# Other tiles for the first block of x and for the feature DFT weights, and the order of the loads with them

## The chip, the cores and the metric

The kernel runs on one NeuronCore of a Trainium2 chip. What counts is the device time of one execution in microseconds (us). Before the change the median of three runs is 1732.21 us (1732.16 to 1733.36).

The engines are TensorE (PE in the profile; PEld is its weight load), VectorE (DVE), ScalarE (ACT) and GpSimd (POOL). SP (SyncE) computes nothing here: it is the one queue from which every DMA of this kernel is issued, in order, and an instruction that waits there holds back all behind it.

## The reference

The input x has 2048 tokens and 640 features. With g = sigmoid(x . gate_w), one number for each token, the result is g * A(x) + (1 - g) * B(x):

```python
# A: real part of a DFT over the features, then over the tokens
a = einsum("bsd,ed->bse", x, dft_hid_re)
b = einsum("bsd,ed->bse", x, dft_hid_im)
y = einsum("ts,bse->bte", dft_seq_re, a) - einsum("ts,bse->bte", dft_seq_im, b)

# B: attention with 32 query heads of 20, one key and one value head
q = (x @ wq).reshape(B, S, 32, 20).transpose(0, 2, 1, 3)
k, v = x @ wk, x @ wv
p = softmax(einsum("bhqd,bkd->bhqk", q, k) * 20 ** -0.5)
o = einsum("bhqk,bkd->bhqd", p, v).transpose(0, 2, 1, 3).reshape(B, S, 640) @ wo
```

All of it is float32.

## The kernel before

**Splits.** A float32 matrix is used as two parts, a high part that TensorE takes fast and the rest. So each loaded tile is *split*: one instruction copies the high part and one subtracts it. In the stage of this change, x and `wq` are split on ScalarE (the copy) and VectorE (the subtraction, `xl` in line 375 and `wql` in line 118); the feature DFT weights `wrT` and `wiT` are split on GpSimd, two instructions for each of two parts (lines 211 and 212). A product is three matmuls (lines 122 to 124).

**The first stage.** It takes the first 100 us or so. The tokens are cut into four blocks of 512 (n = 0 to 3), and the 640 features into five chunks (c) of 128. For each block the stage makes keys, values and the gate's input (`kv`, line 396), then the queries of five groups of heads (`q`, m = 0 to 4). `kv_out` (lines 398 to 412) adds up `kvT`, splits the keys and has them written into `ks` by six small DMAs. `q_out` (lines 382 to 389) splits a bank of queries into `qh` and `ql` and has both stored to DRAM, 256 KB each. There are three buffers of `qh` and three of `ql`, so the fourth `q_out` of a block waits for stores of the first to land. After each `q_out` the split of a chunk of the block after next follows (line 479), and in places some score tiles (`a`, line 251) whose maximum VectorE takes (`mx`, line 258).

In block 0, loads, splits and matmuls go chunk by chunk. Then x of block 1 is loaded and split, `kv_out` and the five `q_out` of block 0 follow, and the loop over blocks 1 to 3 begins. In it, `kv_out` of a block stands on ScalarE and VectorE behind the five `q_out` of the block before, and TensorE needs the bank that it frees for the third group of queries.

**Tiles of x.** `load_x1` takes a tile for a whole block from a pool with two buffers (`xr`): blocks 0 and 2 in one, 1 and 3 in the other. So x of block 2 waits until the last chunk of block 0 is split, and block 3 until the last of block 1.

**Tiles of the DFT weights.** `load_w(i, e)` loads half e of `wrT` (i = 0) or `wiT` (i = 1) in two parts of 480 and 320 KB into two staging tiles that `raw_tile` deals out in turn (`raw0`, `raw1`); chunks 2 and 3 of `wq` used them before, and `xraw`, the x of the second stage (320 KB a tile), uses them after. In the first stage the calls for e = 0 stand at the end of blocks 1 and 2.

**What sets the order.** The instructions of TensorE, ScalarE, VectorE and GpSimd run in the order in which they are written. SP's do not: a scheduler places the DMAs by its own estimate of when tiles come free, and gives a tile whichever buffer of its pool is free first by that estimate. So a load written late can stand early on SP, and hold back what is written before it. `DMAHW0` to `DMAHW7` are eight semaphores that the DMAs take in turn, so that a DMA also waits for the one eight places ahead of it to land.

After the first stage come the products with the feature DFT weights beside score tiles, then the long loop of attention and token DFT, and the output product.

Of the kernel before, what the change touches and what calls it, by code (L numbers as in the profile page):

```python
# [8 lines left out]
F32 = mybir.dt.float32  # L9
F32R = mybir.dt.float32r  # L10
AF = mybir.ActivationFunctionType
ALU = mybir.AluOpType
# [5 lines left out]
P = 128  # L18
# [4 lines left out]
KC = D // P  # L23
# [3 lines left out]
HALF = D // 2  # L27
SJ = NT // 2
SCALE = float(DH) ** -0.5
ROW = 512  # L30
# [3 lines left out]
def kernel(  # L34
# [13 lines left out]
    nc = tc.nc  # L48
# [61 lines left out]
    def words(ap):  # L110
        return ap.bitcast(F32) if ap.dtype == F32R else ap

    def move(dst, src):
        nc.sync.dma_start(words(dst), words(src))  # L114
# [22 lines left out]
    xT_v = xT.rearrange("(c p) t -> p c t", p=P)  # L137
# [18 lines left out]
    def load_qs0(n):  # L156
        if n == 0:
            qs[0] = qbuf[0]
        ts = slice(n * ROW, (n + 1) * ROW)
        for hh in range(2):  # L160
            r = slice(hh * DH, (hh + 1) * DH)
            for k, src in enumerate((qh_d, qh_d, ql_d)):
                b = 64 * hh + 20 * k
                move(qs[0][b : b + 20, ts], src[r, ts])
# [9 lines left out]
    def c_slot(n, shape, dt, name):  # L174
        return cpool.tile(shape, dt, tag=f"c{n}", name=name)
# [6 lines left out]
    def raw_tile(shape, name):  # L182
        nraw["n"] += 1
        k = nraw["n"] % (5 if yp else 2)
        if k >= 2:
            return yp[0].tile(shape, F32, tag=f"raw{k}", name=name, bufs=1)
        return cpool.tile(shape, F32, tag=f"raw{k}", name=name)
# [2 lines left out]
    w_now = {}  # L190
    w_raw = {}

    def load_w(i, e):
        v = (wrT, wiT)[i].rearrange("(c p) n -> p c n", p=P)
        es = slice(e * HALF, (e + 1) * HALF)
        parts = []
        for k, cs in enumerate(CPART):
            shape = [P, cs.stop - cs.start, HALF]
            if k == 0:
                h, l = [c_slot(2 * i + z, shape, F32R, f"w{i}{'hl'[z]}") for z in range(2)]  # L200
            elif i == 1:
                h, l = [c_slot(4 + z, shape, F32R, f"wb{'hl'[z]}") for z in range(2)]
            else:
                h, l = [xp.tile(shape, F32R, name=f"wb{'hl'[z]}0") for z in range(2)]
            raw = raw_tile(shape, "wraw")
            move(raw, v[:, cs, es])
            parts.append((h, l, raw))
        w_raw[i] = parts
# [138 lines left out]
    with ExitStack() as c1:  # L347
        w1 = c1.enter_context(tc.tile_pool(name="w1", bufs=1, side="right"))
        x1 = c1.enter_context(tc.tile_pool(name="x1", bufs=2, side="right"))
# [9 lines left out]
        xs, xsp = {}, {}  # L359

        def load_x1(n, c):
            if n < 4:
                if c == 0:
                    xs[n] = x1.tile([P, KC, ROW], F32, name="xr")
                move(xs[n][:, c], xT_v[:, c, n * ROW : (n + 1) * ROW])

        def split_x1(n, c):
            if n < 4:
                if c == 0:
                    xh = x1.tile([P, KC, ROW], F32R, name="xh")  # L370
                    xl = x1.tile([P, KC, ROW], F32R, name="xl")
                    xsp[n] = (xh, xl)
                xh, xl = xsp[n]
                nc.scalar.activation(xh[:, c], xs[n][:, c], AF.Copy)
                nc.vector.tensor_tensor(xl[:, c], xs[n][:, c], xh[:, c].bitcast(F32), op=ALU.subtract)

        def q_mm(ps, n, m, c):
            ms = slice(m * P, (m + 1) * P)
            xh, xl = xsp[n]
            mm3(ps, wqh[:, c, ms], wql[:, c, ms], xh[:, c], xl[:, c], KC, c)  # L380

        def q_out(ps, n, m):
            ms, ts = slice(m * P, (m + 1) * P), slice(n * ROW, (n + 1) * ROW)
            qh = x1.tile([P, ROW], F32R, name="qh", bufs=3)
            ql = x1.tile([P, ROW], F32R, name="ql", bufs=3)
            nc.scalar.activation(qh, ps, AF.Copy)
            nc.vector.tensor_tensor(ql, ps, qh.bitcast(F32), op=ALU.subtract)
            move(qh_d[ms, ts], qh)
            move(ql_d[ms, ts], ql)

        def kv_mm(ps, n, c):
            xh, xl = xsp[n]
            end = c == KC - 1
            for high in (not end, end):
                m, x = (105, xh) if high else (41, xl)
                nc.tensor.matmul(ps[:m], kvgs[:, c, :m], x[:, c], start=(c == 0 and high), stop=(end and high))
# [17 lines left out]
        def kv_turn(kvT, n, rot):  # L414
            ps = rot(f"kvt_{n}")
            for j in range(4):
                nc.tensor.transpose(
                    ps[:, 64 * j : 64 * j + 41], kvT[:, j * P : (j + 1) * P], ident[:41, :41]
                )
            pv = ps.rearrange("p (j c) -> p j c", c=64)[:, :4]  # L420
            ns = slice(4 * n, 4 * n + 4)
            nc.scalar.activation(vsb[:, ns, :DH], pv[:, :, DH : 2 * DH], AF.Copy)
            nc.vector.tensor_copy(
                gz[:, ns].rearrange("p (j o) -> p j o", o=1), pv[:, :, 2 * DH : 2 * DH + 1]
            )
# [13 lines left out]
        for c in range(KC):  # L439
            if c:  # L440
                load_x1(0, c)
            raw = raw_tile([P, D], "wraw") if c in (2, 3) else w1.tile([P, D], F32, name="wraw", bufs=2)
# [15 lines left out]
        kvT = kv_out(pkv, 0)  # L458
        for m in range(KC):
            q_out(pq[m], 0, m)  # L460
        load_qs0(0)
        rot = Rot(["F1", "V", "S0", "F0"])
        slots = {1: (2, 3), 2: range(KC), 3: range(KC)}
        for n in range(1, 4):
            for c in range(KC):
                load_x1(n + 1, c)
            pkv = rot(f"kv_{n}")
            for c in range(KC):
                kv_mm(pkv, n, c)
            kv_turn(kvT, n - 1, rot)  # L470
            kvT = kv_out(pkv, n)
            if n == 3:
                for k in range(2):
                    load_x(k)
            for m in range(KC):
                ps = rot(f"q_{n}_{m}")
                for c in range(KC):
                    q_mm(ps, n, m, c)
                split_x1(n + 1, m)
                q_out(ps, n, m)  # L480
                if (n, m) == (1, 0):
                    load_qs0(1)
                if m in slots[n]:
                    for z in range(4):
                        a_half(z % 2, f"S{1 + z}")
                if (n, m) == (3, 1):
                    kv_turn(kvT, 3, rot)
                    gate_out()
                if n == 3 and m in (2, 3):
                    split_x(m - 2)  # L490
                if (n, m) == (3, 3):
                    load_x(2)
            if n < 3:
                load_w(n - 1, 0)
                split_w(n - 1)


# [100 lines left out]
    op = ctx.enter_context(tc.tile_pool(name="op", bufs=2))  # L598
# [514 lines left out]
    for plan in plans():  # L1113
        n = sum(w[0] == "b" for w in plan) // 4
# [5 lines left out]
        for what in plan:  # L1120
# [15 lines left out]
            elif what[0] == "b":  # L1136
                p, qh, kc = new[nb[g] // 2]
# [66 lines left out]
```

## Time and profile before

| | before |
|---|---|
| median of 3 runs | 1732.21 us |
| the profiled execution, its own time | 1732.34 us |
| its span, first to last instruction | 1730.6 us |
| TensorE busy | 1710.9 us, 99% |
| VectorE busy | 1381.5 us, 80% |
| ScalarE busy | 1251.2 us, 72% |
| GpSimd busy | 1104.3 us, 64% |
| moved by DMA | 261.47 MB |

The rows of the profile read so. A row of a timeline has start and duration in us, the engine, the line, the operation, the tile it writes and the one it reads, shapes, and in brackets the idle time before it and what ended that. Rows of SP are the issues of DMAs, not the transfers. A row of stretches has the stretch, its length, the busy time of PE, PEld, DVE, ACT and POOL with counts, the granted clock of TensorE (1.00 is full), the DMA share and GB/s. A row of waits has who waited, for what, the sum in us, the number of waits and the longest. The chain of waits follows the work that ended last back from the end; its rows are start, duration and what. A PE row's duration overlaps the next one's: the pace is the distance of the starts.

### The profile page before, as it was taken

How to read it: one execution, taken by the hardware profiler on the slowest of the kernel's cores; microseconds unless marked ns; L12 is line 12 of the kernel's file. 1: busy time of each engine (PE TensorE's matmuls, PEld its weight loads, DVE VectorE, ACT ScalarE, POOL GpSimd, SP SyncE). 2: the span in 40 equal slices, each digit the busy share in tenths (PEclk: the TensorE clock that was granted, in tenths of full speed). 3: DMA queues.
4: the chain of work that ended last, by engine and by line, in shares of the span. 5: the costliest groups of instructions: out<-in, count | busy, mean ns of one | idle time of the engine just before them, and what ended most of it. 6: DMA issues, size and time to landing. Idle time of an engine off the chain costs nothing.

```text
span 1730.6 us, 43337 instructions
## 1 busy us (share of the span) xinstructions
PE 1710.9 (99%) x16752; PEld 1239.4 (72%) x16752; DVE 1381.5 (80%) x2290; ACT 1251.2 (72%) x2543; POOL 1104.3 (64%) x921
## 2 busy tenths in 40 slices
PE   8999999999999999999999999999999999999997
PEld 6686777777677777777777777777777777777664
DVE  5787888888888888888888888888888888888813
ACT  4237888888777677777777777777777767678895
POOL 3045556333356658758777887888877764557785
PEclk9999999999999999999999999999999999999999
DMA  8551223222175556545666776655555533143332
GB/s 270 155 168 56 71 79 105 82 73 72 61 227 168 174 169 196 170 156 200 223 215 211 231 236 217 205 187 185 177 173 170 155 112 111 57 127 117 100 100 85
DMA packets 181499, 261.47 MB, mean 151 GB/s; under 512 B 35696, under 2 KB 136304, under 8 KB 181292
## 3 DMA queue, kind: packets, MB, share of 16 engines
q1 hardware_dynamic: 181292, 258.70, 47.2%
q8 instruction: 132, 2.16, 0.5%
q14 instruction: 75, 0.61, 0.1%
HBM read 184.42 MB, written 76.99 MB: 151 GB/s over the span
## 4 chain that ended last, share of the span: by engine, by line
PE 93%; DMA 2%; DVE 2%; issue 1%; ACT 1%; SPq 1%; POOL 0%; POOLq 0%; DVEq 0%; ACTq 0%
PE av L974 27%; PE y_p L782 21%; PE b L962 18%; PE a L251 15%; PE ab L782 7%; PE oo L782 3%; DVE mx L258 1%; PE q L122 1%; PE q L123 1%; SPq L114 1%; PE q L124 1%; ACT pt L970 1%; DMA wraw<-in_wiT_dram 0%; DMA ql_d<-ql 0%; DMA wraw<-in_wq_dram 0%
## 5 line engine op out<-in xcount | busy, mean ns | idle before, releaser
L258 DVE TENSOR_REDUCE mx<-a 128x1 f32<-128x512 f32 x2048 | 1303.2, 686 | 246.6 <-PE a L251 197.4
L970 ACT ACTIVATE pt<-b 128x512 f32<-128x512 f32 x2048 | 1058.2, 623 | 342.8 <-PE a L251 262.3
L962 PE MATMUL b<-qs,ks 62*128 62x512 f32 x2048 | 755.4, 408 | 3.1 <-ACT pt L970 2.1
L251 PE MATMUL a<-ks,qs 60*128 60x512 f32 x2048 | 707.7, 408 | 2.2 <-DVE mx L258 2.2
L782 PE MATMUL y_p<-tb,ch 64*128 64x320 f32 x3584 | 618.6, 307 | 0.0
L782 PEld LDWEIGHTS y_p<-tb,ch 64*128 64x128 f32 x3584 | 504.3, 186 | 2.9
L974 PE MATMUL av<-pt,vsb 128*32 128x512 f32 x4096 | 485.8, 598 | 0.0
L962 PEld LDWEIGHTS b<-qs,ks 62*128 62x128 f32 x2048 | 345.5, 185 | 187.7 <-DVE mx L258 125.1
L782 PE MATMUL y_p<-tb,cl 64*128 64x320 f32 x1792 | 454.8, 306 | 0.0
L251 PEld LDWEIGHTS a<-ks,qs 60*128 60x128 f32 x2048 | 345.6, 185 | 16.0 <-issue 4.0
L782 PEld LDWEIGHTS y_p<-tb,cl 64*128 64x128 f32 x1792 | 297.2, 186 | 2.7
L974 PEld LDWEIGHTS av<-pt,vsb 128*32 128x32 f32 x4096 | 111.5, 109 | 239.6 <-issue 229.9
L543 POOL TENSOR_TENSOR cl<-craw,ch 128x1024 fp32r<-128x1024 f32 x112 | 268.5, 2397 | 9.0
L824 POOL TENSOR_TENSOR yt<-yt,yu 128x320 f32<-128x320 f32 x86 | 75.0, 872 | 285.3 <-ACT yu L819 232.2
L824 POOL TENSOR_TENSOR abt<-abt,abu 128x320 f32<-128x320 f32 x64 | 55.8, 872 | 198.0 <-ACT abu L819 183.9
L537 POOL TENSOR_TENSOR craw<-craw 128x1024 f32<-128x1024 f32 x64 | 153.4, 2397 | 0.0
L542 POOL CAST ch<-craw 128x1024 fp32r<-128x1024 f32 x112 | 116.6, 1041 | 13.5 <-DMA craw<-in_cre_dram 6.9
L782 PE MATMUL oo<-wo,osp 64*128 64x320 f32 x816 | 91.5, 307 | 0.0
L782 PEld LDWEIGHTS oo<-wo,osp 64*128 64x128 f32 x816 | 86.6, 185 | 1.5
L569 POOL TENSOR_TENSOR tb<-braw,tb 128x320 fp32r<-128x320 f32 x80 | 69.9, 880 | 0.0
L782 PE MATMUL ab<-wbh,xh 64*128 64x320 f32 x256 | 60.1, 306 | 0.0
L782 PE MATMUL ab<-wbh,xl 64*128 64x320 f32 x256 | 59.9, 306 | 0.0
(138 smaller groups left out, 1622.8 us busy)
## 6 DMA issues: line engine op xcount, KB each, us to landing
craw<-in_cre_dram SPq DMA_DIRECT2D x80, 512.0 KB
craw<-in_cim_dram SPq DMA_DIRECT2D x64, 512.0 KB
s_d<-craw SPq DMA_DIRECT2D x32, 512.0 KB
craw<-s_d SPq DMA_DIRECT2D x32, 512.0 KB
braw<-b_d SPq DMA_DIRECT2D x80, 160.0 KB
xraw<-in_xT_dram SPq DMA_DIRECT2D x32, 320.0 KB
b_d<-abt SPq DMA_DIRECT2D x64, 160.0 KB
t_d<-braw SPq DMA_DIRECT2D x64, 160.0 KB
```

Source lines behind the costliest of these rows:

```text
L114: nc.sync.dma_start(words(dst), words(src))
L251: nc.tensor.matmul(ps, qs[v][b : b + 60, qb * P : (qb + 1) * P], ks[b : b + 60, c * ROW : (c + 1) * ROW], start=True, stop=True,)
L258: nc.vector.tensor_reduce(mx[v][:, hh, qb, c : c + 1], ps, axis=AX.X, op=ALU.max)
L537: nc.gpsimd.tensor_tensor(x, raw[0], x, op=how)
L542: nc.gpsimd.tensor_copy(h, x)
L543: nc.gpsimd.tensor_tensor(l, x, h.bitcast(F32), op=ALU.subtract)
L569: nc.gpsimd.tensor_tensor(t[:, 1], raw, t[:, 0].bitcast(F32), op=ALU.subtract)
L782: nc.tensor.matmul(ps, w, x, start=start, stop=stop)
L824: nc.gpsimd.tensor_tensor(t0, t0, t1, op=ALU.add)
L962: nc.tensor.matmul(ps, ks[b : b + 62, kc * P : (kc + 1) * P], qs[NPAIR * (qc // 2) + p][b : b + 62, (qc % 2) * ROW : (qc % 2 + 1) * ROW], ...
L970: nc.scalar.activation(t, ps, AF.Exp, scale=SCALE)
L974: nc.tensor.matmul(ps[32 * g : 32 * g + 32, :], vsb[:, kc, :], t, start=first, stop=last)
```

## The change

There are four edits. The first block's x goes chunk by chunk into buffers of `qh` (chunks 0 to 2) and `ql` (3 and 4), which hold no queries yet. The `xr` pool with its two buffers then serves blocks 1, 2 and 3 and, between them, the e = 0 halves of `wrT` and `wiT`, which leave the staging tiles; both parts of a half share one tile. The loads of block 2 are written ahead of the loop, those of `wrT` and of block 3 at the start of block 1, and those of `wiT` at the start of block 2; the splits of the weights stay where they were. The staging tiles are thereby free for `xraw` from block 0 on.

```diff
--- before.py
+++ after.py
@@ -190,7 +190,7 @@
     w_now = {}
     w_raw = {}
 
-    def load_w(i, e):
+    def load_w(i, e, raws=None):
         v = (wrT, wiT)[i].rearrange("(c p) n -> p c n", p=P)
         es = slice(e * HALF, (e + 1) * HALF)
         parts = []
@@ -202,7 +202,7 @@
                 h, l = [c_slot(4 + z, shape, F32R, f"wb{'hl'[z]}") for z in range(2)]
             else:
                 h, l = [xp.tile(shape, F32R, name=f"wb{'hl'[z]}0") for z in range(2)]
-            raw = raw_tile(shape, "wraw")
+            raw = raws[:, cs, :HALF] if raws is not None else raw_tile(shape, "wraw")
             move(raw, v[:, cs, es])
             parts.append((h, l, raw))
         w_raw[i] = parts
@@ -360,9 +360,13 @@
 
         def load_x1(n, c):
             if n < 4:
-                if c == 0:
-                    xs[n] = x1.tile([P, KC, ROW], F32, name="xr")
-                move(xs[n][:, c], xT_v[:, c, n * ROW : (n + 1) * ROW])
+                if n == 0:
+                    xs[n, c] = x1.tile([P, ROW], F32, tag=("qh", "ql")[c // 3], name="xr0", bufs=3)
+                else:
+                    if c == 0:
+                        xs[n] = x1.tile([P, KC, ROW], F32, tag="xr", name="xr")
+                    xs[n, c] = xs[n][:, c]
+                move(xs[n, c], xT_v[:, c, n * ROW : (n + 1) * ROW])
 
         def split_x1(n, c):
             if n < 4:
@@ -371,8 +375,8 @@
                     xl = x1.tile([P, KC, ROW], F32R, name="xl")
                     xsp[n] = (xh, xl)
                 xh, xl = xsp[n]
-                nc.scalar.activation(xh[:, c], xs[n][:, c], AF.Copy)
-                nc.vector.tensor_tensor(xl[:, c], xs[n][:, c], xh[:, c].bitcast(F32), op=ALU.subtract)
+                nc.scalar.activation(xh[:, c], xs[n, c], AF.Copy)
+                nc.vector.tensor_tensor(xl[:, c], xs[n, c], xh[:, c].bitcast(F32), op=ALU.subtract)
 
         def q_mm(ps, n, m, c):
             ms = slice(m * P, (m + 1) * P)
@@ -381,8 +385,8 @@
 
         def q_out(ps, n, m):
             ms, ts = slice(m * P, (m + 1) * P), slice(n * ROW, (n + 1) * ROW)
-            qh = x1.tile([P, ROW], F32R, name="qh", bufs=3)
-            ql = x1.tile([P, ROW], F32R, name="ql", bufs=3)
+            qh = x1.tile([P, ROW], F32R, tag="qh", name="qh", bufs=3)
+            ql = x1.tile([P, ROW], F32R, tag="ql", name="ql", bufs=3)
             nc.scalar.activation(qh, ps, AF.Copy)
             nc.vector.tensor_tensor(ql, ps, qh.bitcast(F32), op=ALU.subtract)
             move(qh_d[ms, ts], qh)
@@ -458,12 +462,17 @@
         kvT = kv_out(pkv, 0)
         for m in range(KC):
             q_out(pq[m], 0, m)
+        for c in range(KC):
+            load_x1(2, c)
         load_qs0(0)
         rot = Rot(["F1", "V", "S0", "F0"])
         slots = {1: (2, 3), 2: range(KC), 3: range(KC)}
         for n in range(1, 4):
-            for c in range(KC):
-                load_x1(n + 1, c)
+            if n < 3:
+                load_w(n - 1, 0, x1.tile([P, KC, ROW], F32, tag="xr", name="wraw"))
+                if n == 1:
+                    for c in range(KC):
+                        load_x1(3, c)
             pkv = rot(f"kv_{n}")
             for c in range(KC):
                 kv_mm(pkv, n, c)
@@ -491,7 +500,6 @@
                 if (n, m) == (3, 3):
                     load_x(2)
             if n < 3:
-                load_w(n - 1, 0)
                 split_w(n - 1)
```

On the engines that compute, the order of the instructions is the same; only tiles and what is waited for differ. On SP the order differs. Below, `xr_230` and `xr_255` are chunks 3 and 4 of block 0 in their new tiles. From the fourth load of `wq` on to the first write of `ks`, SP stood so before:

```order
L114 DMA wraw<-in_wq_dram 128x640
L114 DMA xr<-in_xT_dram 128x512 x4
L114 DMA wraw<-in_wq_dram 128x640
L114 DMA xr<-in_xT_dram 128x512 x2
L114 DMA wraw<-in_wrT_dram 128x3x320
L114 DMA wraw<-in_wrT_dram 128x2x320
L114 DMA xr<-in_xT_dram 128x512 x10
L114 DMA wraw<-in_wiT_dram 128x3x320
L114 DMA wraw<-in_wiT_dram 128x2x320
L114 DMA ks<-kh 20x512
```

and now:

```order
L114 DMA wraw<-in_wq_dram 128x640
L114 DMA xr_255<-in_xT_dram 128x512
L114 DMA xr<-in_xT_dram 128x512 x3
L114 DMA wraw<-in_wq_dram 128x640
L114 DMA xr<-in_xT_dram 128x512 x7
L114 DMA xraw<-in_xT_dram 128x5x128 x2
L114 DMA wraw<-in_wrT_dram 128x3x320
L114 DMA wraw<-in_wrT_dram 128x2x320
L114 DMA xr<-in_xT_dram 128x512 x5
L114 DMA ks<-kh 20x512
```

The five loads of block 2 and two of `xraw` moved ahead of `wrT`; the five of block 3 stand behind it; `wiT` left this place.

What SP waits for at these places, before, from the first load of block 3 on:

```order
L114 DMA xr<-in_xT_dram 128x512 [waits DMAHW7_49,DVE_49]
L114 DMA xr<-in_xT_dram 128x512 [waits DMAHW0_49]
L114 DMA xr<-in_xT_dram 128x512 [waits DMAHW1_49]
L114 DMA xr<-in_xT_dram 128x512 [waits DMAHW2_49]
L114 DMA xr<-in_xT_dram 128x512 [waits DMAHW3_49]
L114 DMA wraw<-in_wiT_dram 128x3x320 [waits DMAHW4_49,Pool_49]
L114 DMA wraw<-in_wiT_dram 128x2x320 [waits DMAHW5_49,Pool_49]
L114 DMA ks<-kh 20x512 [waits DMAHW6_49,Activation_49]
```

and now, from `wrT` on:

```order
L114 DMA wraw<-in_wrT_dram 128x3x320 [waits DMAHW7_49,DVE_49]
L114 DMA wraw<-in_wrT_dram 128x2x320 [waits DMAHW0_49]
L114 DMA xr<-in_xT_dram 128x512 [waits DMAHW1_49,DMAHW7_49,DMAHW0_49,Pool_49]
L114 DMA xr<-in_xT_dram 128x512 [waits DMAHW2_49]
L114 DMA xr<-in_xT_dram 128x512 [waits DMAHW3_49]
L114 DMA xr<-in_xT_dram 128x512 [waits DMAHW4_49]
L114 DMA xr<-in_xT_dram 128x512 [waits DMAHW5_49]
L114 DMA ks<-kh 20x512 [waits DMAHW6_49,Activation_49]
```

The wait for VectorE (`DVE_49`, at the last split of block 1 in both) moved from the loads of block 3 to `wrT`. The loads of block 3 wait for GpSimd (`Pool_49`, at the fourth instruction on `wrT`): the scheduler gave them the buffer of `wrT`, not that of block 2. The loads of `wiT` now stand behind the last stores of block 1, ahead of the `ks` writes of block 2.

## The prediction, as it was put on record

> **What bounds the kernel now.** I read the page first, then the waits of TensorE over the first 60 us, then the chain of waits there, then the timelines of the engines named in it. The page says that TensorE is the bound:
>
> ```profile
> PE   1710.9 (99%) x16752; PEld 1239.4 (72%) x16752; DVE 1381.5 (80%) x2290; ACT 1251.2 (72%) x2543; POOL 1104.3 (64%) x921
> ```
>
> ```profile
> PE q L122 <- DVE kvT L405: 2.9, 1, 2.9
> ```
>
> With TensorE 99% busy, a change of loads can only pay where TensorE waits. In the first 60 us there is one such wait of size once the matmuls run: 2.9 us for `kvT`. TensorE's own rows show where it stands, and that the clock is low after it:
>
> ```profile
> 35.92 0.39 PE L123 MATMUL q<-xl,wqh 128*128 128x512 f32 x1
> 36.16 0.40 PE L124 MATMUL q<-xh,wql 128*128 128x512 f32 x1
> 39.47 0.56 PE L122 MATMUL q<-xh,wqh 128*128 128x512 f32 x1 [2.92 <-DVE kvT L405]
> 39.83 0.63 PE L123 MATMUL q<-xl,wqh 128*128 128x512 f32 x1
> 40.25 0.63 PE L124 MATMUL q<-xh,wql 128*128 128x512 f32 x1
> ```
>
> ```profile
> 36.30:39.70 3.40, 0.48 (x3) 0.26 (x2) 1.91 (x4) 1.66 (x4) 1.48 (x1) 1.00 1.07 311
> 39.70:43.10 3.40, 3.40 (x9) 2.64 (x9) 3.08 (x6) 2.93 (x6) 0.00 (x0) 0.50 0.86 207
> 135.30:138.70 3.40, 2.74 (x14) 1.01 (x16) 1.29 (x2) 3.40 (x8) 1.60 (x3) 1.00 0.02 5
> 138.70:142.10 3.40, 3.40 (x21) 1.58 (x15) 0.59 (x1) 0.78 (x3) 3.24 (x5) 0.50 0.14 48
> ```
>
> The matmuls start 0.42 us apart (39.83 to 40.25) instead of 0.24 (35.92 to 36.16), and the granted clock (the number before the DMA share) is 0.50 from 39.7 to 43.1. Nine matmuls at some 0.19 extra make 1.7 us. So the stall costs 2.9 + 1.7 = 4.6 us in all, and that is the most that a cure of it could give.
>
> The chain of waits says why `kvT` is late:
>
> ```profile
> 17.90 4.15 DVE xl L375 x2
> 22.07 0.33 SPq L114
> 24.87 8.09 DMA wraw<-in_wiT_dram
> 33.03 3.04 DMA ql_d<-ql
> 36.17 0.70 DVE ql L387
> ```
>
> Read upwards: `kvT` of block 1 stands on VectorE behind the fourth and fifth `ql` of block 0. These need a `ql` buffer, of which there are three, and so the landing of the stores of the first two. The stores stand on the one DMA queue (SP) behind six writes of `ks`, those behind the loads of x for block 3 and of `wiT`, and these behind the last split of block 1. SP's own rows:
>
> ```profile
> 22.07 2.23 SPq L114 DMA_DIRECT2D xr<-in_xT_dram  x5
> 24.39 0.91 SPq L114 DMA_DIRECT2D wraw<-in_wiT_dram  x2
> 25.40 0.91 SPq L114 DMA_DIRECT2D ks<-kh  x1
> 32.19 0.36 SPq L114 DMA_DIRECT2D qh_d<-qh  x1
> 33.03 0.34 SPq L114 DMA_DIRECT2D ql_d<-ql  x1
> 33.97 0.41 SPq L114 DMA_DIRECT2D ql_d<-ql  x1
> ```
>
> The time thus hangs on when SP issues the first store (32.19) and the second `ql_d` store (33.97).
>
> **The change, part by part.** No instruction of an engine is added or taken away; the matmuls and splits stand in the same order. What moves is on SP: x of block 2 no longer waits for a split; two `xraw` loads come forward from 88 us; `wrT` now waits for the last split of block 1 (it takes the buffer of block 1's x); x of block 3 now waits for GpSimd's four instructions on `wrT`, since it got that same buffer and not that of block 2; `wiT` goes back to the end of block 1. All ten instructions queued behind the wait on GpSimd wait with it: four more loads of x, then the six writes of `ks`, and then the stores. This is the added wait that decides, and I follow the steps to it.
>
> Step 1, the last split of block 1.
>
> ```profile
> 17.90 1.48 DVE L375 TENSOR_TENSOR xl<-xr,xh 128x512 fp32r<-128x512 f32 x1
> 19.30 2.74 DVE L375 TENSOR_TENSOR xl<-xr,xh 128x512 fp32r<-128x512 f32 x1
> 17.34 1.50 POOL L211 CAST w0h<-wraw 128x960 fp32r<-128x960 f32 x1 [12.43 <-DMA wraw<-in_wrT_dram]
> 18.92 2.58 POOL L212 TENSOR_TENSOR w0l<-wraw,w0h 128x960 fp32r<-128x960 f32 x1
> 22.70 1.57 POOL L212 TENSOR_TENSOR wbl<-wraw,wbh 128x640 fp32r<-128x640 f32 x1
> 63.88 0.68 DVE L375 TENSOR_TENSOR xl<-xr,xh 128x512 fp32r<-128x512 f32 x1
> ```
>
> While GpSimd splits `wrT`, the last two splits took 1.48 and 2.74 us instead of 0.68. With `wrT` not yet there, that overlap is gone: from 17.90 two splits, the second 0.6 behind, end at 19.2 instead of 22.04. This is a gain of 2.8 us for whatever waits for it, and now that is `wrT`.
>
> Step 2, `wrT` lands. The DMA engines were full from 9 us until 20.6:
>
> ```profile
> DMA  9999999999999999999999999999999854000000
> ```
>
> (40 slices of 0.35 us from 9 us on.) In place of the 800 KB of `wrT` the queue now holds 640 KB of `xraw` ahead of it, so it is full to about 20.5 again. [...] Bounds: 21.5 if the backlog is gone at 20; 24 if the small rows of `xraw` hold the engines 1.5 us longer.
>
> Step 3, GpSimd. Its four instructions on `wiT` had no split beside them:
>
> ```profile
> 32.18 0.99 POOL L211 CAST w1h<-wraw 128x960 fp32r<-128x960 f32 x1 [7.90 <-DMA wraw<-in_wiT_dram]
> 36.24 1.54 POOL L212 TENSOR_TENSOR wbl<-wraw,wbh 128x640 fp32r<-128x640 f32 x1
> ```
>
> They took 37.78 - 32.18 = 5.6 us; those on `wrT` took 24.27 - 17.34 = 6.9 with the splits beside them. At 22.4 no splits are left, so I take 5.6: done at 28.0. The bounds are 27.1 and 30.9.
>
> Step 4, SP. Five loads of x (22.07 to 24.30: 2.2 us, 2.3 with the gap behind) and six writes of `ks`. The latter took 32.19 - 25.40 = 6.8 with waits for landings in them, and 4.8 in block 3, where the queue was quiet:
>
> ```profile
> 83.41 0.77 SPq L114 DMA_DIRECT2D ks<-kh  x1
> 88.18 0.99 SPq L114 DMA_DIRECT2D xraw<-in_xT_dram  x2
> ```
>
> I take 4.9: the landings they wait for are now those of x alone, not of `wiT`. The first store goes at 28.0 + 0.1 + 2.3 + 4.9 = 35.3, against 32.19.
>
> Step 5, from the stores to TensorE. The second `ql_d` store went 33.97 - 32.19 = 1.8 us after the first store, of which 0.5 was a wait for the landing of `wiT`; now 1.3, at 36.6. Its landing released this:
>
> ```profile
> 37.97 0.69 DVE L387 TENSOR_TENSOR ql<-q,qh 128x512 fp32r<-128x512 f32 x1 [1.12 <-DMA ql_d<-ql]
> 38.65 0.67 DVE L405 TENSOR_TENSOR kvT<-kv,kvl 41x512 f32<-41x512 f32 x1
> ```
>
> From store to `ql` 4.0 us, from `ql` to the matmul 39.47 - 37.97 = 1.5. TensorE resumes at 36.6 + 4.0 + 1.5 = 42.1: **2.6 us later** than now. With the lower bounds throughout (27.1, `ks` in 4.8, a landing in the 3.0 us of the chain's row), it resumes at 40.1, which is still 0.6 later; with the upper ones (30.9, 6.1 for `ks`) at 46, 6.5 later.
>
> Step 6, the clock. If the low stretch begins and ends at the same places, 39.7 to 43.1 is now nearly empty (1 us of work), like 36.3 to 39.7 was, and the low clock lasts one stretch more, to 46.5: from 42.1 that is 4.4 us at half speed, 2.2 lost instead of 1.7. I take +0.4. Bounds: -0.7, if it resumes early enough that 43.1 stays the end, and +1.7 for one more whole stretch.
>
> [...]
>
> What costs nothing:
>
> ```profile
> 43.00:102.00 59.00, 58.93 (x263) 41.00 (x262) 43.29 (x76) 15.45 (x29) 3.14 (x2) 1.00 0.56 171
> 65.24 0.69 DVE L387 TENSOR_TENSOR ql<-q,qh 128x512 fp32r<-128x512 f32 x1 [0.68 <-ACT qh L386]
> 107.67 0.31 PE L782 MATMUL ab<-w1h,xh 64*128 64x320 f32 x1
> ```
>
> The two `xraw` loads, early by 70 us, delay only `wrT` behind them (counted). `wiT` goes out at about 58 us and is split by 67, long before its first use at 107.67. Its split now meets the x splits of block 3: an `xl` as late as the 2.74 us one above comes 2 us late, VectorE has 0.68 us idle ahead of the next `ql`, and the rest is caught up over the next groups while TensorE works from its other banks. Without that cover it would cost up to 2 us. TensorE is busy 58.93 of the 59 us from 43 to 102, so no slack there takes up what block 1 loses: it reaches the end whole.
>
> Sum: +2.6 + 0.4 = +3.0 on the profiled execution, 1732.34 us (span 1730.6), thus 1735.3; that execution stands 0.1 above the median of 1732.21, so I say **1735.2**.
>
> **Rivals.** (a) It does what its words say: loads follow the splits, and stall and dip go: -4.6, **1727.6**. For it: x of block 2 and `wiT` leave the path, and the split ends 2.8 us earlier. Against it: for no stall the stores must go 2.9 us earlier, at 29.3, so GpSimd must be done by 22.0, before `wrT` has landed. It decides if x of block 3 is not held by GpSimd on the chip.
>
> (b) The loss is there but is paid back by the clock: the dip at 138.7 follows a piece of 3.4 us in which TensorE waits on banks. Shifted by 2.6 us against the stretches, that wait falls across two of them, and no dip follows: -1.7, so +1.3, **1733.5**. For it, a wait that falls across two stretches brings no dip now:
>
> ```profile
> 105.10 0.49 PE L251 MATMUL a<-ks,qs 60*128 60x512 f32 x1 [1.55 <-DVE mx L258]
> 104.60:108.00 3.40, 2.90 (x34) 2.90 (x35) 3.40 (x7) 0.27 (x1) 0.00 (x0) 1.00 0.48 159
> ```
>
> Against it, the same shift can put this wait whole into one stretch and bring a dip.
>
> (c) Slower by more: the small rows of `xraw` and their queue make `wrT` land at 24, GpSimd takes 6.9 and the dip lasts a stretch more: 4.7 + 1.7 = +6.4, **1738.6**. It decides from a first store at 37 us on.
>
> **How the numbers follow.** Forecast 0.62, with a range of its own of 1733.4 to 1737.0 (steps 2 to 4 half way to their bounds); (a) 0.07; (b) 0.13; (c) 0.18. A measurement of this kernel can tell about 0.2%, 3.5 us, from no change: faster ends at 1728.7, slower begins at 1735.7. The forecast's range lies 0.38 above 1735.7. Slower: 0.62 x 0.38 + 0.18 = 0.41; faster 0.07; within 0.52. The range leaves out (a) and the top of (c): 1731.5 to 1739.5.
>
> **What would show it.** Right: the last split of block 1 ends near 19.2; the first GpSimd cast starts near 22.4; SP's loads of x for block 3 start near 28, with GpSimd as what they waited for; the first `qh_d` store goes after 34; TensorE's wait for `kvT` grows from 2.9 to some 5.5 us, with a clock of 0.50 behind it. Wrong: a first store before 32, a shorter wait for `kvT`, or a new wait of TensorE past 43 us.

## The result, and the profile after

The changed kernel takes 1738.19 us (median of seven runs, 1736.86 to 1739.53). The kernel before, run between them, takes 1733.36 (seven runs, 1731.56 to 1734.43). The ratio is 1.0033, with a 95% interval from 1.0024 to 1.0042: the change costs 0.33%, some 4.8 us. The forecast was 1735.2; the time lies in the range that was given, above the forecast's own range (1733.4 to 1737.0), and where rival (c) was priced, at 1738.6.

The profiled execution of the changed kernel took 1739.53 us (span 1737.7), the longest of the seven; that of before took 1732.34 (span 1730.6). So the two traces lie 7.1 us apart, more than the medians.

The page of the changed kernel, then the waits of TensorE in its first 60 us:

```profile
PE 1713.3 (99%) x16752; PEld 1239.9 (71%) x16752; DVE 1382.0 (80%) x2290; ACT 1250.6 (72%) x2543; POOL 1102.7 (63%) x921
```

```profile
PE q L122 <- DVE kvT L409: 7.7, 1, 7.7
```

TensorE still waits in the same place and for the same thing, but 7.7 us instead of 2.9. No wait was cured. Its timeline after that wait, and the stretches of the low clock (stretch, length, busy time of PE, PEld, DVE, ACT, POOL, then the granted clock):

```profile
44.49 0.76 PE L122 MATMUL q<-xh,wqh 128*128 128x512 f32 x1 [7.66 <-DVE kvT L409]
45.06 0.63 PE L123 MATMUL q<-xl,wqh 128*128 128x512 f32 x1
45.48 0.63 PE L124 MATMUL q<-xh,wql 128*128 128x512 f32 x1
...
50.49 0.74 PE L251 MATMUL a<-ks,qs 60*128 60x512 f32 x4
```

```profile
39.60:49.90 10.30, 5.41 (x13) 4.31 (x14) 5.81 (x10) 5.18 (x10) 0.00 (x0) 0.51 0.89 233
...
145.40:148.90 3.50, 3.50 (x23) 1.74 (x17) 0.72 (x2) 0.81 (x3) 3.34 (x5) 0.54 0.11 38
148.90:1737.70 1588.80, 1578.35 (x15977) 1137.63 (x15973) 1282.12 (x2126) 1196.87 (x2439) 1059.57 (x871) 1.00 0.47 148
```

TensorE resumes at 44.49 (39.47 before: 5.0 us later), and the clock stays low (a granted 0.50) until 49.6 (43.1 before; the first row of stretches runs 0.3 us past the end of the low clock). From 148.9, behind the second low stretch, to the end the changed kernel needs 1588.8 us; the piece of before behind its second low stretch is 1588.5 (142.1 to 1730.6). So nearly all of the loss is made ahead of 149 us.

The chain of waits of the changed kernel between 18 and 31 us, without the rows under 0.1 us:

```profile
18.49 1.30 DVE xl L379 x2
19.80 4.19 DMA wraw<-in_wrT_dram
...
24.05 0.99 POOL w0h L211
...
25.12 2.27 POOL w0l L212
27.39 1.13 POOL wbh L211
...
28.59 1.57 POOL wbl L212
30.18 0.34 SPq L114
```

And SP's issues, in order:

```profile
15.21 1.06 SPq L114 DMA_DIRECT2D xraw<-in_xT_dram  x2
19.80 0.90 SPq L114 DMA_DIRECT2D wraw<-in_wrT_dram  x2
30.18 2.24 SPq L114 DMA_DIRECT2D xr<-in_xT_dram  x5
32.51 0.89 SPq L114 DMA_DIRECT2D ks<-kh  x1
...
37.35 0.42 SPq L114 DMA_DIRECT2D qh_d<-qh  x1
```

Read it downwards. `wrT` waits for the last split of block 1 (to 19.79), lands 4.2 us after its issue, GpSimd splits it until 30.15, and only then can SP issue the loads of x for block 3. Between 20.70 and 30.18 SP issues nothing. The six writes of `ks` and the stores of the queries stand behind: the first store goes at 37.35 instead of 32.19.

**Where the 6.4 us are.** A wait of 1.55 us on a bank of scores stands in both kernels behind the first stage, and can serve as a mark. In before its row starts at 105.10 (quoted in the prediction). In the changed kernel:

```profile
111.54 0.49 PE L251 MATMUL a<-ks,qs 60*128 60x512 f32 x1 [1.55 <-DVE mx L258]
```

So 6.44 us are lost up to the mark; the other 0.7 us by which the two spans differ lie behind it, and what they are is open. The first score group behind the stall starts at 50.49, in before at 44.68:

```profile
44.68 0.80 PE L251 MATMUL a<-ks,qs 60*128 60x512 f32 x4
73.16 0.74 PE L251 MATMUL a<-ks,qs 60*128 60x512 f32 x4
```

That is 5.81: 5.02 of later resumption, 0.79 of longer low clock. The remaining 0.63 is at one place, the group that answers to the second of those rows. TensorE, VectorE and GpSimd of the changed kernel:

```profile
74.61 1.37 PE L251 MATMUL a<-ks,qs 60*128 60x512 f32 x4
```

```profile
69.67 2.77 DVE L379 TENSOR_TENSOR xl<-xr,xh 128x512 fp32r<-128x512 f32 x1
...
72.96 2.47 DVE L258 TENSOR_REDUCE mx<-a 128x1 f32<-128x512 f32 x4
```

```profile
69.63 2.27 POOL L212 TENSOR_TENSOR w1l<-wraw,w1h 128x960 fp32r<-128x960 f32 x1
```

The four score tiles take 1.37 us instead of 0.74, because the maxima of the group before (72.96, four in a row) come late. They come late because the split of x ahead of them took 2.77 us: it started 0.04 us after GpSimd's 2.27 us on `wiT` and ended 0.54 us after it, 0.68 being its usual time. No row of the waits shows this, since the four score tiles are one row of the timeline.

### The profile page after: what moved, and what is told of

It reads as the page before. It is cut to its first block, busy times and chain, and to the rows that moved or that the text cites. A ratio compares the mean times of both kernels' runs of the same rounds, so it can differ in the third digit from the quotient of the medians.

```text
span 1737.7 us, 43337 instructions
## 1 busy us (share of the span) xinstructions
PE 1713.3 (99%) x16752; PEld 1239.9 (71%) x16752; DVE 1382.0 (80%) x2290; ACT 1250.6 (72%) x2543; POOL 1102.7 (63%) x921
## 4 chain that ended last, share of the span: by engine, by line
PE 93%; DVE 2%; DMA 2%; SPq 1%; ACT 1%; issue 1%; POOL 0%; POOLq 0%; ACTq 0%; DVEq 0%
PE av L982 27%; PE y_p L790 21%; PE b L970 18%; PE a L251 15%; PE ab L790 7%; PE oo L790 3%; DVE mx L258 1%; SPq L114 1%; DMA wraw<-in_wq_dram 1%; PE q L122 1%; DMA qh_d<-qh 1%; ACT pt L978 0%; PE q L123 0%; PE q L124 0%; DVE xl L379 0%
```

## The experiments

Eight kernels ran, in two groups of four (the order of the table); the runs of before that go with the first group have a median of 1732.14 us, those with the second 1731.77, those with the change 1733.36. So kernels of different groups are compared by their distance from before. "The mark" is the start of the row with the 1.55 us wait of above. No clock dip behind it enters it, but it is one execution's number: the transposes at the head of block 1 alone start between 28.6 and 30.5 us in these executions, so differences of a us in this column mean little by themselves.

| kernel | median, us | ratio to before, 95% | mark, us | against before's 105.10 |
|---|---|---|---|---|
| the change | 1738.19 | 1.0033 (1.0024 to 1.0042) | 111.54 | +6.4 |
| q tiles only | 1731.99 | 1.0002 (0.9993 to 1.0011) | 105.95 | +0.9 |
| weights only | 1737.62 | 1.0029 (1.0017 to 1.0040) | 109.49 | +4.4 |
| weights late | 1730.44 | 0.9994 (0.9985 to 1.0003) | 104.06 | -1.0 |
| double split | 1744.55 | 1.0073 (1.0057 to 1.0088) | 118.23 | +13.1 |
| filler | 1736.84 | 1.0029 (1.0018 to 1.0041) | 111.62 | +6.5 |
| before, stores first | 1731.33 | 0.9994 (0.9985 to 1.0003) | 105.46 | +0.4 |
| stores first | 1728.42 | 0.9981 (0.9972 to 0.9990) | 101.67 | -3.4 |
| stores first, qs | 1727.08 | 0.9972 (0.9960 to 0.9983) | 101.66 | -3.4 |

The theory was that of the prediction: the loads of x for block 3 wait for GpSimd's split of `wrT`, and everything behind them on SP waits too. The rivals to tell it from: that the earlier loads of block 2 and of `xraw` do the harm, by filling the DMA queue; and that the clock carries a part of the loss.

### One part of the change alone: the tiles of block 0

The first block's x goes into the `qh` and `ql` buffers; `wrT` and `wiT` stay in the staging tiles and are loaded at the end of their blocks, as before the change.

```diff
         for n in range(1, 4):
-            if n < 3:
-                load_w(n - 1, 0, x1.tile([P, KC, ROW], F32, tag="xr", name="wraw"))
-                if n == 1:
-                    for c in range(KC):
-                        load_x1(3, c)
+            if n == 1:
+                for c in range(KC):
+                    load_x1(3, c)
...
             if n < 3:
+                load_w(n - 1, 0)
                 split_w(n - 1)
```

> Only the first part of the change: block 0 of x in the qh and ql buffers, the weights in their old staging tiles and with their loads written where they were. Theory: wrT goes out near 15 us and lands near 20; its split on GpSimd ends near 26 and holds wiT, which stands ahead of the ks writes: first store at 31 to 33, as in the kernel before (32.2), a wait for kvT of 2 to 3.5 us with one low stretch: 1731.5 to 1734. Rival (the early loads of block 2 are what costs, by filling the DMA engines): as slow as the change, 1737 or more.

Measured: 1731.99 us, the same as before. Its wait for `kvT`, and SP:

```profile
PE q L122 <- DVE kvT L409: 3.5, 1, 3.5
```

```profile
19.40 3.13 SPq L114 DMA_DIRECT2D xr<-in_xT_dram  x5
24.21 3.19 SPq L114 DMA_DIRECT2D wraw<-in_wiT_dram  x2
...
32.37 0.42 SPq L114 DMA_DIRECT2D qh_d<-qh  x1
```

The loads of block 2 without a wait cost nothing that can be measured, but gain nothing either. The loads of block 3 go out 2.7 us earlier than before (19.40 against 22.07). Then `wiT` holds SP until 27.4, because its staging tiles come free only when GpSimd has split `wrT`, and the first store is at 32.37, where it was. So the early loads of block 2 are not what costs.

### The other part alone: the weights in x's buffers

Block 0 keeps its tile in the `xr` pool; `wrT` and `wiT` take tiles there by turns.

```diff
             if n < 4:
-                if n == 0:
-                    xs[n, c] = x1.tile([P, ROW], F32, tag=("qh", "ql")[c // 3], name="xr0", bufs=3)
-                else:
-                    if c == 0:
-                        xs[n] = x1.tile([P, KC, ROW], F32, tag="xr", name="xr")
-                    xs[n, c] = xs[n][:, c]
+                if c == 0:
+                    xs[n] = x1.tile([P, KC, ROW], F32, tag="xr", name="xr")
+                xs[n, c] = xs[n][:, c]
```

> Only the second part of the change: the weights in the buffers of x, block 0 of x in such a buffer too. Theory: x of block 3 still gets the buffer of wrT and waits for GpSimd until about 30 us; four of its loads instead of five stand ahead of the ks writes: first store near 37, wait for kvT about 7 us, three low stretches: 1736.5 to 1738.5, nearly all of the change's loss. Rival (first block's tiles are the cause): 1733 or less.

Measured: 1737.62 us, ratio 1.0029. This part carries nearly all of the loss. Its profiled execution was the shortest of its six (1734.49), so its trace shows the least of it:

```profile
PE q L122 <- DVE kvT L406: 4.8, 1, 4.8
```

```profile
28.89 1.76 SPq L114 DMA_DIRECT2D xr<-in_xT_dram  x4
...
35.67 0.42 SPq L114 DMA_DIRECT2D qh_d<-qh  x1
```

Four loads of x leave at 28.89, when GpSimd is done, then the `ks` writes, then the first store, at 35.67. Stores and wait came out smaller than expected, by 1.3 and 2.2 us; the place and the order are those of the theory.

### The same tiles, with the weights loaded one block later

This takes the wait on GpSimd away: the loads of block 3 are written first, and `wrT` and `wiT` follow one block later, so that no load of x stands behind a split of weights in block 1. GpSimd runs the same instructions, but its splits of the weights move back by a block with their loads.

```diff
         for n in range(1, 4):
-            if n < 3:
-                load_w(n - 1, 0, x1.tile([P, KC, ROW], F32, tag="xr", name="wraw"))
-                if n == 1:
-                    for c in range(KC):
-                        load_x1(3, c)
+            if n == 1:
+                for c in range(KC):
+                    load_x1(3, c)
+            else:
+                load_w(n - 2, 0, x1.tile([P, KC, ROW], F32, tag="xr", name="wraw"))
...
                 if (n, m) == (3, 1):
+                    split_w(1)
...
-            if n < 3:
-                split_w(n - 1)
+            if n == 2:
+                split_w(0)
```

> The halves of wrT and wiT are loaded one block later than in the change (at the start of blocks 2 and 3), so x of block 3 takes the buffer of block 1 with no GpSimd work in between, and neither weight stands ahead of the stores of block 0. Theory (what SP must issue ahead of the first store sets TensorE's wait): block 3's loads go from 19.8 us to 22, the writes of ks as soon as the keys are there, 25.2 to 30.1, the first store at 30.1 instead of 37.35; TensorE's wait for kvT falls from 7.7 to under 1 us and no low clock follows: about 1729 us, 4 below the kernel before and 9 below the change. Rival (the stores land late because the DMA engines are full, whatever SP's order): the wait stays above 2 us, 1732 or more.

Measured: 1730.44 us, 1.4 above what was expected; the loss is gone, the ratio to before is 0.9994 (0.9985 to 1.0003). SP and TensorE's waits:

```profile
20.32 3.40 SPq L114 DMA_DIRECT2D xr<-in_xT_dram  x5
...
30.11 0.43 SPq L114 DMA_DIRECT2D qh_d<-qh  x1
```

```profile
PE a L251 <- DMA qs<-ql_d: 1.1, 1, 1.1
PE q L122 <- DVE kvT L409: 0.8, 1, 0.8
PE kv L400 <- DVE xl L379: 0.6, 1, 0.6
```

The first store is where it was expected, 7.2 us earlier than in the change and 2.1 earlier than in before. The wait for `kvT` is down to 0.8, and the granted clock is 1.00 in every stretch from 1 to 160 us. Yet of the 4.6 us that stall and dip made up in before, only 1.0 is gained at the mark. A part has turned into new waits, 1.1 us for the queries that are loaded back (`qs`) and 0.6 for a split of x; 0.54 is again a score group behind a late split of x (1.28 us instead of 0.74; the split at 62.32 took 2.66 us instead of 0.68, beside GpSimd's 2.25 us from 62.18 on). The loads of block 2 and of `xraw` stand as early on SP here as in the change (`xraw` at 15.72 us), and the loss is gone all the same: the rival that they do the harm is out.

### Twice the suspected wait

GpSimd splits `wrT` twice, with the same result; all else is the change.

```diff
             if n < 3:
+                if n == 1:
+                    for part in w_raw[0]:
+                        low_part(*part)
                 split_w(n - 1)
```

> The change with GpSimd's split of wrT done twice (the same values written again), which doubles the time for which block 3's x is held. The scheduler then puts four of its five loads behind the stores. Theory: GpSimd is done near 36.2 us instead of 30.2, one load and six ks writes follow, the first store goes near 41.6 instead of 37.35: TensorE's wait for kvT grows by 4.2 us to about 11.9, and the time by 3.5 to 6: 1741.5 to 1744. Rival (the landing of stores, not GpSimd, sets it): no change, 1738.

Measured: 1744.55 us, 0.6 above the range that was expected. SP and the waits:

```profile
35.95 0.34 SPq L114 DMA_DIRECT2D xr<-in_xT_dram  x1
...
41.24 0.48 SPq L114 DMA_DIRECT2D qh_d<-qh  x1
```

```profile
PE q L122 <- DVE kvT L409: 12.1, 1, 12.1
PE kv L400 <- DVE xl L379: 2.5, 1, 2.5
```

GpSimd is done at 35.9 instead of 30.15, and the stall of TensorE grows by 4.4 us. It does not grow by the whole 5.8, because the scheduler now puts four of the five loads of block 3 behind the stores; only one is left in front. Those loads then come too late for their own block: the second row of waits, 2.5 us. That GpSimd's end sets the stores' time is the theory, and this run bears it out; the rival forecast no change.

### Is the low clock a part of the loss?

Thirty matmuls whose result nobody reads stand in front of the one that stalls, so that TensorE is busy through the wait.

```diff
             for m in range(KC):
+                if (n, m) == (1, 2):
+                    fill = bank("S1", "fill")
+                    for _ in range(30):
+                        nc.tensor.matmul(fill, wqh[:, 0, :P], xsp[1][0][:, 0], start=True, stop=True)
                 ps = rot(f"q_{n}_{m}")
```

> The change, with 30 matmuls of 512 columns whose result nobody reads put on TensorE just ahead of the matmul that waits for kvT: at 0.235 us apart they take 7.0 us of a wait of 7.7, and compute nothing that is used. Theory (the low clock after the stall is a separate cost that comes from TensorE's idleness): the wait shrinks to under 1 us, the clock stays full behind it, and the time falls by the 2.3 to 2.7 us that the low stretches cost: 1735.5 to 1736 against 1738.2 of the change. Rival (the low clock costs nothing at the end, since something later takes up the slack): 1738, no change.

Measured: 1736.84 us, ratio 1.0029, within the interval of the change itself. The gain that was expected did not come, although the granted clock is 1.00 from 10 us to the end of the first stage. TensorE:

```profile
44.39 0.47 PE L122 MATMUL q<-xh,wqh 128*128 128x512 f32 x1 [1.20 <-DVE kvT L409]
...
49.46 1.23 PE L251 MATMUL a<-ks,qs 60*128 60x512 f32 x4 [1.33 <-DMA qs<-ql_d]
...
61.49 0.43 PE L400 MATMUL kv<-xl,kvgs 128*41 128x512 f32 x1 [0.90 <-DVE xl L379]
...
111.62 0.50 PE L251 MATMUL a<-ks,qs 60*128 60x512 f32 x1 [1.56 <-DVE mx L258]
```

TensorE resumes at the same time as in the change (44.39 against 44.49), works at full pace (0.23 us from start to start, against 0.43 in the change), and then waits 1.33 us for `qs` and 0.90 for a split of x, two waits that the change does not have. At the mark it stands at 111.62, the change at 111.54. So the change's slow matmuls (12 at some 0.19 us extra, 2.3 us) cost nothing in the end: while they ran, the queries came back. The loads of `qs` were issued at nearly the same times in both (the last at 47.61 and 47.69). What bounds the first stage there is the row of stores and loads on SP, not TensorE's pace. Against the runs of before on its own chip the filler stands at +5.1 us, the change at +4.8.

### Is it the place of the stores?

If the time of the first stores sets the stage, putting them ahead of other work on SP should gain, in before too. In the kernel before, the `ks` writes of block 0 are written behind its first six stores:

```diff
-            for r0 in (0, 64):
-                move(ks[r0 : r0 + 20, ts], kh)
-                move(ks[r0 + 20 : r0 + 40, ts], kl)
-                move(ks[r0 + 40 : r0 + 60, ts], kh)
+            def put():
+                for r0 in (0, 64):
+                    move(ks[r0 : r0 + 20, ts], kh)
+                    move(ks[r0 + 20 : r0 + 40, ts], kl)
+                    move(ks[r0 + 40 : r0 + 60, ts], kh)
+            if n:
+                put()
+            else:
+                put_ks.append(put)
...
             q_out(pq[m], 0, m)
+            if m == 2:
+                put_ks[0]()
         load_qs0(0)
```

> The kernel before with one thing changed: five of the six writes of ks of block 0 are issued behind its first six stores, not ahead of them. Theory (the SP queue ahead of the stores sets the wait for kvT, also in the kernel before): first store near 26.5 us instead of 32.2; the second ql_d store lands by 34.5, so TensorE does not wait for kvT at 36.6; 3 to 4.5 us gained, 1728 to 1729. Rival (the stores land late because block 3's x and wiT fill the DMA engines): the wait stays at 2 us or more and the time at 1731.5 or more.

Measured: 1731.33 us, ratio 0.9994 (0.9985 to 1.0003): no gain that can be told. SP and TensorE:

```profile
25.87 0.97 SPq L114 DMA_DIRECT2D ks<-kh  x1
26.94 0.58 SPq L114 DMA_DIRECT2D qh_d<-qh  x1
```

```profile
43.25 0.47 PE L251 MATMUL a<-ks,qs 60*128 60x512 f32 x1 [2.46 <-DMA qs<-ql_d]
```

Five of the six writes did go behind the stores, and the first store left at 26.94 instead of 32.19. The wait for `kvT` fell from 2.9 to 0.8 us. In its place came a wait of 2.46 us for `qs`. A low stretch (a granted 0.50) follows that wait too, from 44.4 to 47.9. The wait moved by one step along the same queue; the mark is at 105.46.

The same edit on top of "weights late":

> The change with its weights one block later (as in weights_late) and, on top, five of the six ks writes of block 0 behind the first six stores. Theory: first store near 26.2 us, no wait for kvT; the loads of qs for the first scores, which TensorE waited for 1.1 us in weights_late, go 1 to 3 us sooner and are in time: 1728 to 1729. Rival (what is left in weights_late is not of this queue): as weights_late, 1730.4.

Measured: 1728.42 us, ratio 0.9981 (0.9972 to 0.9990), faster than before. The first store on SP, the first score group, and the one low stretch of the first 160 us (a granted 0.50 from 135.3 to 137.0):

```profile
26.39 0.38 SPq L114 DMA_DIRECT2D qh_d<-qh  x1
```

```profile
40.27 1.26 PE L251 MATMUL a<-ks,qs 60*128 60x512 f32 x4
```

```profile
135.40:138.90 3.50, 3.50 (x21) 1.42 (x15) 0.43 (x1) 0.60 (x2) 3.34 (x5) 0.55 0.13 47
```

Here the wait for `kvT` is gone. Of that for `qs` some 0.5 us are left inside the first score group (1.26 us instead of 0.74; a weight load of TensorE waits 0.37 for `qs` there), and TensorE still waits 0.6 for a split of x. The mark is at 101.67: 3.4 us gained, the same as the medians say (1728.42 against 1731.77). Neither edit alone did this: late weights left a wait of 1.1 us on `qs`, early stores one of 2.46.

At last, in addition, the loads of `qs` are written ahead of the last two pairs of stores:

```diff
             if m == 2:
                 put_ks[0]()
+                load_qs0(0)
         for c in range(KC):
             load_x1(2, c)
-        load_qs0(0)
```

> As stores_first, with the loads of qs for block 0 ahead of the last two pairs of stores, which they do not need. Theory: qs is there well before TensorE asks for it near 40 us; no wait at all in the first stage: 1727.5 to 1728.5. Rival (the late last stores then hold the queries of block 1): a wait for a bank near 45 us, 1729 or more.

Measured: 1727.08 us, ratio 0.9972 (0.9960 to 0.9983). This is the lowest time of all, 4.7 us under before, where the change was 4.8 above its own. Its first score group no longer waits for `qs`, nor its block 2 for a split of x:

```profile
41.55 0.74 PE L251 MATMUL a<-ks,qs 60*128 60x512 f32 x4
```

What this last edit adds to the time is not shown: the mark stands at 101.66, where "stores first" has it, and the intervals of the two overlap. The traces leave room for a gain: block 1 began 1.45 us later in this execution than in that of "stores first" (transposes at 30.50 against 29.05), and at those of block 2 both stand level (52.59 and 52.61). In its profiled execution the clock is full at the place where the kernel ahead of it has the dip:

```profile
135.40:138.90 3.50, 3.50 (x40) 2.59 (x33) 1.93 (x4) 2.11 (x5) 3.34 (x5) 1.00 0.14 47
```

## Why the prediction was right, and where it was short

The side, the mechanism and its place were right: x of block 3 got the buffer of `wrT`, waits for GpSimd on SP, and holds the stores back. Three runs bear on that: without that wait (weights late) the loss is gone, with GpSimd's work doubled the stall grows, and the half of the change that brings the wait brings the loss. But the sum was short: +3.0 was forecast, and the traces show +6.4 up to the mark, the medians +4.8. Of the 3.0 us between 1735.2 and 1738.19, 1.15 are the kernel before, which stood at 1732.21 in the three runs of the forecast and at 1733.36 in all seven. The outcome had not been given the largest chance: a time from 1735.7 on, which came, had 0.41, one within 3.5 us of before 0.52. By its steps:

| step | forecast | measured |
|---|---|---|
| 1, last split of block 1 ends | 19.2 | 19.79 |
| 2, first cast of `wrT` starts | 22.4 | 24.05 |
| 3, GpSimd on `wrT` | 5.6, until 28.0 | 6.1, until 30.15 |
| 4, five loads and six `ks` writes on SP | 7.2, first store 35.3 | 7.17, first store 37.35 |
| 5, first store to TensorE | 6.8, resumes 42.1 | 7.14, resumes 44.49 |
| 6, low clock ends | 46.5, +0.4 | 49.6, +0.79 |
| split of `wiT` in block 3 | 0 (2 without cover) | 0.63 |

Of the 2.4 us by which TensorE resumed later than forecast:

- **0.6 is the start.** The fifth chunk of `wq` was issued at 9.37 us, in before at 8.76, with the same loads ahead of it; the split of block 1 is as much later. This time was 9.22 in "before, stores first", whose loads are those of before up to there, so most of the 0.6 can be the execution's. A share of the change is not excluded: the six kernels with both of its parts lie at 9.17 to 9.90, the four others at 8.70 to 9.22.
- **1.0 is step 2, the term that was mis-sized most.** From its issue `wrT` took 4.19 us to land instead of 3.2. The prediction had the bound for it (24, if the small rows of `xraw` hold the engines longer) and took the value near the lower end. The backlog was not longer than forecast: the engines move 153 GB/s from 21 to 22 us, 374 in the next us, and 3 from 24 to 27.9. The data of `wrT` thus came behind a lull, and when the first cast started nearly all of both parts (800 KB) had come over, where the forecast counted the first part's 480 KB. From the end of the backlog at 20.5 to its 22.4 the forecast counts, beside the time of these 480 KB, a term that no run shows; the runs show the time from issue to landing as a whole, the 4.19 us above. Why the data came so late is not shown, but that `xraw` is the reason is unlikely: "weights only" has `xraw` on the queue earlier (11.11), and its first cast still starts 3.73 us after its issue of `wrT` (22.89 against 19.16).
- **0.5 is step 3.** "No splits are left" was true of x, but a split of the keys stood there: it took 2.42 us instead of 0.68, and GpSimd's cast beside it 1.19 instead of 0.72 (last section).
- **0.3 is step 5.** Step 4 was right to 0.03 us.

**Step 6** was wrong in its reason more than in its size. The extra 0.79 is there, but the filler shows that the dip is not a cost to be added to the stall: without it the same time goes into waits for `qs` and for x. The sentence that stall and dip make 4.6 us, "the most that a cure of it could give", adds up two prices that, behind the change's stall, did not add; rival (a)'s price of -4.6 had the same error. At the mark no cure reached 4.6. Weights late took stall and dip away and gained 1.0 at the mark; it took the order of the stores as well to gain 3.4.

**What costs nothing:** the cover for the split of `wiT` was not whole. The prediction saw the place, a split of x as late as 2.74 us, and held the rest to be caught up; TensorE lost 0.63 at 74.6, a small case of the "new wait of TensorE past 43 us" that the prediction named as a sign of being wrong. `wiT` itself went out at 62.2 and was split by 74.7, not at 58 and by 67. That the loss reaches the end whole was right: no later row gives any back.

**Rivals.** (a) did not come: GpSimd held x of block 3. (b) did not come in this execution: the dip is there, at 145.2 instead of 138.7. That the place of a wait against the stretches decides on a dip was the author's reading of two rows, and no run shows it. (c) came closest: `wrT` at 24, a first store behind 37 and a dip one stretch longer were its conditions, and all three were measured. GpSimd's 6.9 us were not (6.1), and the dip's 1.7 us were not its price; later stores, the start and the split of `wiT` made up for that. Its 1738.6 is 0.4 us from the median, and that is in part luck: its sum is only partly the same, its base was 1.15 us lower, and its own conditions do not give its 4.7. `wrT` 1.6 us and GpSimd 1.3 us longer than in the forecast put 2.9 on the 2.6, so 5.5, and 1739.4 by its sum. As a difference from before, its +6.4 and the forecast's +3.0 lie about equally far from the +4.8 of the medians.

**Open:** the traces differ by 7.1 us, the medians by 4.8. The profiled execution of the change is the longest of its seven and starts 0.6 late, and 0.7 of its distance lie behind the mark; where the clock dips fall in the others cannot be seen.

## What to carry to other kernels

Where one queue issues all DMAs in order, a load that waits for an engine costs what stands behind it on the queue (here the first store, 37.35 us instead of 32.19): count these, and ask for the first whose landing somebody needs. A tile pool with more kinds of tenants can hand a load the buffer of the slowest one (here x of block 3 that of `wrT`, free at 30.15), so read from the order which tenant it waits for. A stall of TensorE and its clock dip do not say what a cure gives: when the queue is the bound, the wait reappears at the next thing that comes over it (2.9 us for `kvT` became 0.8, and 2.46 for `qs`, in "before, stores first"). Here only moving both, the loads of weights and the stores, gained.

## What the runs showed of the hardware that was not expected

**Low clock in stretches of some 3.4 us, at another place in each kernel.** The granted clock was 0.50 in them. Low stretches in the first stage lasted 3.4, 6.8 or 10.2 us, and began at 38.4, 39.4, 39.7, 41.3, 41.4 and 44.4 us in six of the kernels above. Between the starts of two of one execution lay 99.0 us in before (29 times 3.41), 105.8 in the change (31 times 3.41) and 27.3 in "double split" (8 times 3.41). In the change TensorE was busy for 0.94 of the 3.50 us from 35.9 to 39.4; then, at the low clock, for 0.00 of 3.40 us (39.4 to 42.8), 1.71 of 3.40 (42.8 to 46.2) and 3.40 of 3.40 (46.2 to 49.6), and from 49.6 on the clock was full (1.00 from 49.9 to 110). What went ahead of a low stretch was not the same each time: in before TensorE was busy for 0.48 of 3.40 us ahead of that at 39.7, and for 2.74 of 3.40 ahead of that at 138.7, while 2.45 of 3.50 us (101.1 to 104.6) had a full clock behind them (1.00 from 104.6 to 108.0). What decides it is not shown here. Behind the first stage the same piece of work gives a dip in some profiled executions (138.7 in before, 135.1 in "stores first") and none in others ("stores first, qs", "weights late"). A dip of 3.4 us can cost some 1.7 (nine matmuls at 0.19 in before), and that is of the order of the spread of a kernel's runs (before: 1731.56 to 1734.43), though no trace shows two executions of one kernel.

**A VectorE subtraction beside a GpSimd instruction can take longer, and not only for x.** The split of the keys in the changed kernel, beside GpSimd's second instruction on `wrT` (25.12 to 27.39 in the chain), and the same kind of instruction 20 us later with GpSimd idle:

```profile
25.51 2.42 DVE L411 TENSOR_TENSOR kl<-kvT,kh 20x512 fp32r<-20x512 f32 x1 [0.70 <-ACT kh L410]
45.04 0.68 DVE L411 TENSOR_TENSOR kl<-kvT,kh 20x512 fp32r<-20x512 f32 x1 [0.69 <-ACT kh L410]
```

It took 2.42 us instead of 0.68, on 20 rows, and ended at 27.93, 0.54 us behind GpSimd's. GpSimd pays as well: its next cast started at 27.32, ahead of that end, and took 1.19 us; in before, at 35.44, with no split on VectorE beside it, the same cast took 0.72:

```profile
27.32 1.19 POOL L211 CAST wbh<-wraw 128x640 fp32r<-128x640 f32 x1
```

```profile
35.44 0.72 POOL L211 CAST wbh<-wraw 128x640 fp32r<-128x640 f32 x1
```

In three pairs of the changed kernel the instruction that started second ended late: the 2.77 us at 69.67 and the 2.42 at 25.51 each 0.54 us behind GpSimd's, the cast's 1.19 at 27.32 0.58 behind VectorE's. Why they do is not shown. The maxima that VectorE took beside GpSimd's last instruction on `wiT`, from a bank of scores, were not held up (2.47 us for four, 0.62 apart).
